# First pair of batches: order of one x load, of two copies and of four vector sums changed

## The chip, the cores and the metric

The kernel runs on one core of one Trainium2 chip. The metric is the device time of one execution in microseconds. The core has five engines that run side by side, each with a queue of its own: PE multiplies matrices into PSUM, DVE, ACT and POOL do elementwise work, SP only issues DMAs. An instruction waits in its queue until what it needs is there, and all behind it on that engine wait too.

## The reference

```python
def _attn_ref(x, state):                     # x (8,8,512,64), state (8,8,32,64)
    scores = scale * np.matmul(x, state.transpose(0, 1, 3, 2))
    ...                                      # softmax over the last axis
    xread = np.matmul(a, state)
    scores2 = scale * np.matmul(state, x.transpose(0, 1, 3, 2))
    ...                                      # softmax over the last axis
    sread = np.matmul(a2, x)
    return np.concatenate([xread, sread], axis=2)

def _moe_ref(x, w_in, w_out):                # w_in (512,2048), w_out (2048,512)
    h = x @ w_in
    g = h * np.cos(h)
    return (g @ w_out).astype(np.float32)
```

The attention's result, 544 rows of 512 numbers for each of eight batches, goes row by row through the second function. The two weight matrices arrive as float64, so the kernel gets them as pairs of 32-bit words.

## The kernel before

**Tiles and steps.** The order of all work is written out by hand. The main loop (line 1283) goes through 16 steps for each of the eight batches, and 16 more for the rows of the states. A step makes one tile: 128 of the 2048 columns of h for one batch's 512 rows. Its parts are `hidden` (PE, the matmuls of h, line 490), `gate` (ACT, a rounding of h, line 560), `gate2` (DVE, q, line 563), `gate3` (ACT, the cosine as a sine, line 566) and `gate4` (DVE, the product g = h cos h, line 580). Batches go in pairs of 32 steps. In the first 28 steps h goes to two PSUM banks in turn, so `hidden` of a step needs `gate4` of two steps before. `first_pair` (line 1186) is the order of a step in these; `later_pair` is that of the steps after.

**A batch's attention** is spread over the steps by `plan` (lists `pe`, `x_act`, `y_act`, `x_dve`, `y_dve`, `z_act`, which `first_pair` and `later_pair` call as `go(0)` to `go(5)`). It turns x (`tokens`), forms scores, maxima, exponentials and sums, spreads and normalizes them, turns the second softmax (`turn`, PE into the banks `at`; `turn_kept`, ACT, PSUM to SBUF), and reads x with it (`reads`, then `keep` on DVE). For batch 0, `turn` stands in step 1 and `reads` in steps 2 and 3. `reads` is the last to need the x of its batch in `x_b`: with it the loads of the next batch's x become due (line 478), and `load_now` (line 128) issues them on SP at the end of the step.

**Weights.** Eighteen loads bring float64 weights into three buffers in turn (`fetch`, SP, line 212). `convert` makes float32 of each in parts: "1" and "2" on ACT (lines 243 and 246), "b" and "c" on DVE (249 and 252), "f" on POOL (257), which also issues the load that can follow (a buffer is free after "c"). Step 0 has conversion 4, step 1 conversion 5, and so on (`conv_at`).

**Products with seven multiplications.** From step 29 on, h times w_out is made with seven block products in place of eight, twice nested. That needs sums of weights and of gates:
- inner sums of seven weight matrices (`inner_weights`, POOL, line 681). Each also sends its matrix (`send_raw`, line 669) and its four sums (line 684) to HBM with SP, and `fetch_block` (line 700) reads them back block by block; the first three at step 24. The last of the seven, matrix `SQ`, is itself a difference of two weight matrices, made by `weight_sum` on DVE in two halves (L1108, 128x1024 each, at the ends of steps 22 and 25), and its `inner_weights` stands in step 25.
- outer sums of gates (`outer_sum`, through `sub`, line 709), in halves `half` and pieces `i`. On DVE a piece is one instruction of 128x1024, on POOL two of 128x512. For the first pair, `mid_at` puts a sum into the middle of a step (after `go(3)`), `outer_at` at its end. The sum `o=0, x1=0, x2=2` has half 0 in steps 25 and 26 (`mid_at`) and half 1 at the ends of steps 26 and 28, all on DVE.
- inner sums of gates for each product (`Product.sums`, POOL, line 709), in steps 27 to 29 for the first.
- sums of the attention's weights (`sw_sums`, POOL, line 523), which the seven products of h (line 540) need from step 30 on; POOL does them after the first two of those inner sums of gates.

`warm` (line 938) is matmuls of zeros that PE does while it would wait.

Of the kernel before, what the change touches and what calls it, by code (L numbers as in the profile page):

```python
# [13 lines left out]
ALU = mybir.AluOpType  # L14
# [8 lines left out]
def kernel(  # L23
# [55 lines left out]
    def matrix(n):  # L79
        return quad(n).rearrange("p t (u d) -> p (t u) d", d=HD)  # L80
# [142 lines left out]
    def convert(i, parts):  # L223

        for p in parts:
            if p == "f":
                if i not in (1, 2) and i + 3 < N_LOADS:  # L230
                    fetch(max(i + 4, 6))
            elif f64:
                convert_part(i, p)
# [30 lines left out]
    class Attention:  # L264
# [144 lines left out]
                                    in_=self.z2[:, j, P * c:P * c + P],  # L409
                                    identity=ident)  # L410

        def turn_kept(self, j):
            nc.scalar.copy(self.a2T[:, j].rearrange("p c m -> p (c m)"),
                           at[j])

# [557 lines left out]
    def plan(b):  # L975
        pe, x_act, y_act, x_dve, y_dve, z_act = [
            {s: [] for s in range(NF)} for _ in range(6)]

        def prod(s, b, nt, *bank):
            pe[s].append((b, "products", nt) + bank)  # L980
            x_act[s].append((b, "products_kept", nt) + bank)

        def pairs(s, b, name, kept, i):
            pe[s] += [(b, name, i), (b, name, i + 1)]
            x_act[s].append((b, kept, i))
            y_act[s].append((b, kept, i + 1))

        def early(b, s):
            if b == 1:
                pairs(s[0], b, "tokens", "tokens_kept", 0)  # L990
                pairs(s[1], b, "tokens", "tokens_kept", 2)
            else:
                for k in range(NK):
                    to = (x_dve, y_dve)[k % 2]
                    to[s[k // 2]].append((b, "tokens_turned", k))
            pe[s[2]].append((b, "scores"))
            x_dve[s[2]].append((b, "max1"))
            x_dve[s[3]].append((b, "spread1"))
            y_dve[s[3]].append((b, "shift"))
            if b == 1:  # L1000
                x_dve[s[4]].append((b, "max2"))
                y_act[s[4]].append((b, "exps"))
            else:
                y_dve[s[4] - 1].append((b, "max2"))
                z_act[s[4]].append((b, "exps"))
            if b == 1:
                x_dve[s[5]].append((b, "sums"))
                y_dve[s[5]].append((b, "spread1"))
                x_dve[s[6]].append((b, "norm1"))
            else:  # L1010
                y_dve[s[4]].append((b, "sums1"))
                x_dve[s[5]].append((b, "spread2"))
                y_dve[s[5]].append((b, "norm1"))

        def late(b, s):
            pairs(s[0], b, "turn", "turn_kept", 0)
            pe[s[1]].append((b, "reads", 0))
            pe[s[2]].append((b, "reads", 1))
            x_dve[s[2]].append((b, "keep"))
            if len(s) > 3:  # L1020
                turned(b, s[3])

        def turned(b, s):
            pe[s].append((b, "keep2"))
            x_act[s].append((b, "keep3"))


        if b == 0:
            pe[0].append((0, "products", 0, SIDE, HC, WC))
            y_dve[0] += [(0, "products_taken", 0, SIDE, HC, WC),  # L1030
                         (0, "inverse2")]
            prod(7, 0, 2, SIDE)
            prod(11, 0, 3)
            prod(13, 1, 0, SIDE)
            late(0, (1, 2, 3, 4))
            early(1, (5, 6, 7, 8, 9, 10, 11))
            late(1, (12, 13, 14))
        else:
            bank = (SIDE,) if b == 1 else ()
            if b == 1:  # L1040
                turned(1, 0)
            prod(0, b, 1, *bank)
            prod(3, b, 2, *bank)
            prod(8, b, 3, *bank)
            if b + 1 < B:
                prod(12, b + 1, 0)
                early(b + 1, (1 + (b == 1), 2 + (b == 1), 4, 5, 7, 8, 9))
                late(b + 1, (9, 10, 11, 15))
        return pe, x_act, y_act, x_dve, y_dve, z_act
# [6 lines left out]
    for i, t in enumerate(all_tiles):  # L1056
        t.mate = all_tiles[i ^ 1]
    pairs = [all_tiles[2 * NF * n].pair for n in range(B // 2)]
    stage_at, sums_at, outer_at, mid_at, weights_at = [
        defaultdict(list) for _ in range(5)]  # L1060
    PERIOD, STAGES = 2 * NF, len(ORDER)
    ROWS = {"p1": 0, "p2": 1, "p5": 0, "p3": 3, "p6": 0, "p7": 2, "p4": 1}

# [23 lines left out]
    for n in range(B // 2):  # L1087
        end = n == B // 2 - 1
        for r, engine, o, x1, x2, half in (
                ((25, 26), dve, 0, 2, 0, 0),  # L1090
                ((27 - (not n), 28), dve, 0, 2, 0, 1), ((31, 31), pool, 2, 3, 2, 0), ((33, 33), dve, 0, 3, 0, 0),
                ((34, 34 + (not end)), dve, 0, 3, 0, 1),
                ((35, 36), dve, 2, 3, 2, 1),
                ((38 - end,) * 2, pool, 1, 1, 0, 0),
                ((39 - end,) * 2, pool, 1, 1, 0, 1)):
            for i in range(2):
                at_ = mid_at if n == 0 and r[i] < 27 and r[0] == 25 else outer_at
                at_[PERIOD * n + r[i]].append(
                    (engine, n, o, x1, x2, half, i))

# [31 lines left out]
            0, a11, temps[0], (i,), () if i < 3 else (16,) * 4))  # L1132
    for steps, o, x1, x2, op in (
            ((18, 19), A21, A11, A21, ALU.subtract),
            ((22, 25), SQ, A12, A22, ALU.subtract)):
        for i in range(2):
            weights_at[steps[i]].append(
                lambda o=o, x1=x1, x2=x2, op=op, i=i: weight_sum(
                    o, x1, x2, op, i))

# [5 lines left out]
    for at_, what in (  # L1146
            (15, lambda: send_raw(0, a11)),
            (17, lambda: send_raw(2, a22)),
            (19, lambda: send_raw(1, a12)),
            (15, lambda: quads_free.append(10)),  # L1150
            (16, lambda: pool_sum(SQ, A21, A22, ALU.add)),
            (17, lambda: quads_free.append(9)),
            (17, lambda: inner_weights(3, matrix(SQ), temps[1])),
            (18, lambda: pool_sum(A22, SQ, A11, ALU.subtract)),
            (20, lambda: inner_weights(5, matrix(A21), temps[0])),
            (22, lambda: inner_weights(4, matrix(A22), temps[1])),
            (23, lambda: quads_free.append(A11)),
            (25, lambda: inner_weights(6, matrix(SQ), temps[0])),
            (25, lambda: quads_free.append(A21)),
            (27, lambda: quads_free.append(A22)),  # L1160
            (27, lambda: quads_free.append(TEMPS)),
            (28, lambda: quads_free.append(SQ))):
        weights_at[at_].append(what)
# [18 lines left out]
    def go(n):  # L1182
        for p in todo[n]:
            part(*p)

    def first_pair(step, t):
        last, conv = conv_at.get(step - 1, -1), conv_at.get(step, -1)
        if step == 4:
            warm(1, acc[0])
        if step != 1:  # L1190
            hidden(t)
        if step == 0:
            hidden(all_tiles[1])
            warm(3, acc[0])
            gate(t)
            gate2(t)
            convert(3, "bcdf")
            convert(4, "1")
            go(0)
        else:  # L1200
            go(0)
            if step == 5:
                states(1, side_banks[0])
            gate(t)
            gate2(t)
            if step == 3:
                warm(4, acc[0])
                part(0, "products", 1, SIDE)
            go(1)
            go(3)  # L1210
            for what in mid_at[step]:
                outer_sum(*what)
            if step == 1:
                convert(4, "bcdf")
            elif last >= 0 and step < 5:
                convert(last, "bcdf")
            if conv >= 0 and not todo[1]:
                convert(conv, "1")
        gate3(t)
        go(5)  # L1220
        if step == 3:
            part(0, "products_kept", 1, SIDE)
        gate4(t)
        if step == 6:
            states_kept(1, side_banks[0])
        if last >= 0 and 4 < step < 11:
            convert(last, "bcdf")
        if conv >= 0 and todo[1] and step > 0:
            convert(conv, "1")
        go(2)  # L1230
        if conv >= 0:
            convert(conv, "2")
        if step > 10 and conv >= 0 and not todo[1]:
            convert(conv, "bcdf")
        go(4)
        if step > 10 and conv >= 0 and todo[1]:
            convert(conv, "bcdf")
# [126 lines left out]
```

## Time and profile before

| | us |
|---|---|
| median of 9 runs (lowest, highest) | 743.95 (743.48, 745.67) |
| the profiled execution | 744.91 |
| its span in the profile | 743.1 |
| PE busy | 713.1 |
| POOL busy | 538.9 |
| DVE busy | 498.2 |
| ACT busy | 338.7 |

The rows below have, per stretch of the profile, each engine's busy time:

| stretch, us | steps | PE | DVE | ACT | POOL |
|---|---|---|---|---|---|
| 24 to 60 | 0 to 6 | 34.34 | 24.63 | 30.80 | 14.35 |
| 60 to 104 | 7 to 16 | 38.93 | 37.45 | 36.71 | 23.88 |
| 104 to 126 | 16 to 22 | 20.93 | 18.61 | 10.33 | 20.80 |
| 126 to 160 | 22 to 30 | 27.87 | 29.23 | 18.49 | 24.44 |
| 160 to 220 | 30 to 41 | 58.34 | 44.62 | 29.53 | 56.01 |

A timeline row gives start, duration, engine, line, operation, tile written and tiles read, shape, count, and in brackets the idle time before it with the engine and line that ended it. Times are from the start of the span. TensorE's granted clock is at full speed (0.999 of it) throughout.

### The profile page before, as it was taken

The page shows a single profiled execution, that of the slowest core. Times are in us where ns is not written, and L with a number is a line of the kernel's source. Part 1 is how long each engine was busy: PE and PEld are TensorE (multiplying, and loading weights), DVE is VectorE, ACT ScalarE, POOL GpSimd, SP SyncE. Part 2 cuts the span into 40 slices and gives each one's busy share as a digit, 9 for nine tenths or more (in the row PEclk, how much of TensorE's full clock was granted, in tenths as well). Part 3 has the DMA queues.
Part 4 walks back from the last instruction along what each step waited for, and adds up shares of the span by engine and source line. Part 5 has one row for each costly group of instructions (what it writes and reads, how often), then busy time and mean ns, then how long its engine had stood idle before and what let it go on. Part 6 is the DMA issues. An engine that isn't in the chain of part 4 may idle for free.

```text
span 743.1 us, 10759 instructions
## 1 busy us (share of the span) xinstructions
PE 713.1 (96%) x3624; PEld 519.8 (70%) x3624; DVE 498.2 (67%) x707; ACT 338.7 (46%) x562; POOL 538.9 (73%) x528
## 2 busy tenths in 40 slices
PE   8999989799999999999999999999999999999997
PEld 4443333367767878777777778777688788888886
DVE  4768779876975658859766587869656457355550
ACT  3777873644373446344634454443734433211110
POOL 1345469598998997497998765779989665799600
PEclk9999999999999999999999999999999999999999
DMA  9495399977245964692237725762325466455662
GB/s 252 148 257 202 133 242 304 315 158 166 76 127 116 212 157 132 143 194 83 86 86 149 177 86 112 144 170 72 75 73 122 114 201 143 111 155 195 166 149 43
DMA packets 212470, 112.39 MB, mean 151 GB/s; under 512 B 158336, under 2 KB 175232, under 8 KB 212416
## 3 DMA queue, kind: packets, MB, share of 16 engines
q1 hardware_dynamic: 211328, 111.19, 57.8%
q8 instruction: 29, 0.48, 0.3%
q10 hardware_dynamic: 960, 0.39, 0.2%
q14 instruction: 25, 0.20, 0.1%
q0 software_dynamic: 128, 0.13, 0.1%
HBM read 88.08 MB, written 23.59 MB: 150 GB/s over the span
## 4 chain that ended last, share of the span: by engine, by line
PE 57%; POOL 22%; DVE 8%; ACT 4%; DMA 4%; issue 3%; SPq 1%; POOLq 0%; DVEq 0%; ACTq 0%
PE o L762 29%; POOL g_all L709 17%; PE h L540 13%; PE h L490 5%; POOL swS_all L523 3%; PE at L328 3%; PE at L863 2%; DMA x_b<-in_x_dram 2%; POOL sw L523 2%; DVE g_all L709 2%; PE at L425 2%; PE o L938 1%; DVE q_all L563 1%; PE o L863 1%; DVE g_all L580 1%
## 5 line engine op out<-in xcount | busy, mean ns | idle before, releaser
L709 POOL TENSOR_TENSOR g_all<-g_all 128x512 f32<-128x512 f32 x256 | 336.4, 1344 | 55.2 <-DVE g_all L709 40.1
L762 PE MATMUL o<-g_all 128*128 128x256 f32 x1456 | 344.0, 381 | 2.4 <-POOL g_all L709 2.4
L762 PEld LDWEIGHTS o<-g_all 128*128 128x128 f32 x1456 | 273.8, 190 | 49.2 <-issue 5.5
L563 DVE TENSOR_TENSOR q_all<-q_all,h 128x1024 f32<-128x1024 int32 (+1 forms) x88 | 85.5, 971 | 48.6 <-ACT q_all L560 48.4
L566 ACT ACTIVATE q_all<-q_all,halfpi 128x1024 f32<-128x1024 f32 (+1 forms) x88 | 84.1, 956 | 54.9 <-DVE q_all L563 54.8
L560 ACT ACTIVATE q_all<-h 128x1024 int32<-128x1024 f32 (+1 forms) x88 | 73.2, 831 | 77.6 <-PE h L540 35.1
L580 DVE TENSOR_TENSOR g_all<-h,q_all 128x1024 f32<-128x1024 f32 (+1 forms) x88 | 85.7, 973 | 26.7 <-ACT q_all L566 24.8
L549 DVE TENSOR_TENSOR h<-h,sums_all 128x256 f32<-128x256 f32 x96 | 41.2, 429 | 76.1 <-PE h L540 58.2
L490 PE MATMUL h<-aT,sw 128*128 128x512 f32 x128 | 61.6, 605 | 10.9 <-DVE g_all L580 10.2
L540 PE MATMUL h<-aS_all,swS_all 128*128 128x256 f32 x192 | 60.3, 396 | 3.2 <-ACT sums_all L544 1.8
L540 PE MATMUL h<-aT,sw 128*128 128x256 f32 x192 | 59.6, 392 | 3.8 <-DVE g_all L580 3.4
L540 PE MATMUL h<-aS_all,sw 128*128 128x256 f32 x192 | 58.0, 384 | 0.1
L709 DVE TENSOR_TENSOR g_all<-g_all 128x1024 f32<-128x1024 f32 x40 | 57.1, 1444 | 0.1
L540 PEld LDWEIGHTS h<-aS_all,swS_all 128*128 128x128 f32 x192 | 33.9, 189 | 27.9 <-issue 11.2
L490 PEld LDWEIGHTS h<-aT,sw 128*128 128x128 f32 x128 | 22.8, 189 | 43.3 <-DVE g_all L580 19.3
L767 ACT COPY o<-o 128x256 f32<-128x256 f32 x26 | 9.3, 357 | 85.3 <-PE o L762 85.3
L257 POOL TENSOR_TENSOR w_in<-w_in,aS_all 128x1024 int32<-128x1024 int32 (+1 forms) x10 | 19.3, 1927 | 37.9 <-DVE w_in L252 17.9
L540 PEld LDWEIGHTS h<-aT,sw 128*128 128x128 f32 x192 | 34.5, 190 | 16.3 <-DVE g_all L580 12.1
L523 POOL TENSOR_TENSOR swS_all<-sw 128x128 f32<-128x128 f32 x48 | 22.8, 474 | 29.2 <-ACT sw L461 29.2
L540 PEld LDWEIGHTS h<-aS_all,sw 128*128 128x128 f32 x192 | 35.6, 190 | 8.3 <-DVE h L549 2.7
L773 ACT COPY o<-sums_all 128x256 f32<-128x256 f32 x26 | 9.8, 378 | 68.9 <-PE o L762 68.9
L603 DVE SCALAR_TENSOR_TENSOR held<-o,held 128x512 f32<-128x512 f32 x40 | 27.1, 680 | 13.7 <-PE o L762 13.1
(115 smaller groups left out, 919.7 us busy)
## 6 DMA issues: line engine op xcount, KB each, us to landing
g_all<-blocks_kept SPq DMA_DIRECT2D x206, 256.0 KB, 2.9
blocks_kept<-g_all SPq DMA_DIRECT2D x48, 256.0 KB, 3.4
g_all<-in_moe_w_out_dram SPq DMA_DIRECT2D x8, 1024.0 KB, 5.0
out_dram<-ot SPq DMA_DIRECT2D x128, 64.0 KB, 2.0
g_all<-in_moe_w_in_dram SPq DMA_DIRECT2D x6, 1024.0 KB, 5.6
xT<-in_x_dram SPq DMA_DIRECT2D x96, 64.0 KB, 3.0
x_b<-in_x_dram SPq DMA_DIRECT2D x24, 256.0 KB, 4.8
x_b<-in_x_dram SPq DMA_DIRECT2D x16, 128.0 KB, 4.4
```

Of the source, the lines that this page charges most:

```text
L328: nc.tensor.matmul(out=(to or at)[j][Ns * k:Ns * k + Ns, n0:n1], lhsT=w[D * j:D * j + D, self.b, Ns * k:Ns * k + Ns], rhs=r(slice(D * j, D ...
L490: nc.tensor.matmul(out=t.hp, lhsT=t.lhs(i), rhs=t.rhs(i), start=(i == 0), stop=(i == t.kn - 1))
L523: nc.gpsimd.tensor_tensor(o, x1, x2, op=op)
L540: nc.tensor.matmul(out=out_, lhsT=w, rhs=r, start=start, stop=True, skip_group_check=True)
L549: nc.vector.tensor_tensor(o, h2[:, LO], sums_all[:, 0], op=ALU.add)
L560: nc.scalar.activation(t.q.bitcast(I32), t.hp, func=ACTF.Copy, bias=0.25)
L563: nc.vector.tensor_tensor(t.q, t.q.bitcast(I32), t.hp, op=ALU.subtract)
L566: nc.scalar.activation(t.q, t.q, func=ACTF.Sin, bias=halfpi, scale=-TWO_PI)
L580: nc.vector.tensor_tensor(g, t.hp, t.q, op=ALU.mult)
L603: nc.vector.scalar_tensor_tensor(out=out.t[:, ch], in0=bank, scalar=TWO_PI, in1=b.t[:, ch], op0=ALU.mult, op1=ALU.add)
L709: engine.tensor_tensor(o[:, i:i + n], x1[:, i:i + n], x2[:, i:i + n], op=ALU.subtract)
L762: nc.tensor.matmul(out=o, lhsT=ring[(self.first + k) % NB][:, i], rhs=g[:, i], start=(start and i == 0), stop=(i == QT - 1), skip_group_ch ...
```

## The change

Four edits, all for the first pair of batches:

1. At step 3 `load_now(H)` stands right after `go(0)`, where `reads` of batch 0 has just been issued, and not only at the end of the step. On SP the eight loads of batch 1's x now stand ahead of weight load 9 (into w_out), not behind it.
2. For batch 0 the turned weights are copied out of PSUM by DVE (`turn_taken`), not by ACT. On DVE the first copy stands between `gate2` and conversion 4's part "b" of step 1, the second behind `gate4` of step 1. On ACT conversion 5's part "1" now stands ahead of step 1's sine.
3. The two halves of the last `weight_sum` move to step 23: the first into the new list `idle_at`, which is called behind `gate4` and ahead of `go(4)` (the reduction of the exponentials, `sums1`), the second to the end of step 23. The `inner_weights` that reads them, with its four DMAs (`send_raw`), moves from step 25 to 24, ahead of the first three block fetches on SP; its four sums on POOL follow those of matrix 4, as before.
4. Half 1 of the outer sum `o=0, x1=0, x2=2` goes from DVE (ends of steps 26 and 28) to POOL (end of step 25), there four instructions of 128x512 behind the last `inner_weights` and ahead of the first inner sums of gates.

PE has the same instructions in the same order.

```diff
-        def turn_kept(self, j):
-            nc.scalar.copy(self.a2T[:, j].rearrange("p c m -> p (c m)"),
-                           at[j])
+        def turn_kept(self, j, copy=None):
+            (copy or nc.scalar.copy)(
+                self.a2T[:, j].rearrange("p c m -> p (c m)"), at[j])
+
+        def turn_taken(self, j):
+            self.turn_kept(j, nc.vector.tensor_copy)
...
         def late(b, s):
-            pairs(s[0], b, "turn", "turn_kept", 0)
+            if b == 0:
+                pe[s[0]] += [(b, "turn", 0), (b, "turn", 1)]
+                x_dve[s[0]].append((b, "turn_taken", 0))
+                y_dve[s[0]].append((b, "turn_taken", 1))
+            else:
+                pairs(s[0], b, "turn", "turn_kept", 0)
...
+    idle_at = defaultdict(list)
...
-                ((27 - (not n), 28), dve, 0, 2, 0, 1), ((31, 31), pool, 2, 3, 2, 0), ((33, 33), dve, 0, 3, 0, 0),
+                ((27, 28) if n else (25, 25), dve if n else pool, 0, 2, 0, 1),
+                ((31, 31), pool, 2, 3, 2, 0), ((33, 33), dve, 0, 3, 0, 0),
...
-                at_ = mid_at if n == 0 and r[i] < 27 and r[0] == 25 else outer_at
+                at_ = (mid_at if n == 0 and r[0] == 25 and engine is dve
+                       else outer_at)
...
-            ((22, 25), SQ, A12, A22, ALU.subtract)):
+            ((23, 23), SQ, A12, A22, ALU.subtract)):
         for i in range(2):
-            weights_at[steps[i]].append(
+            (idle_at if o == SQ and i == 0 else weights_at)[steps[i]].append(
...
-            (25, lambda: inner_weights(6, matrix(SQ), temps[0])),
+            (24, lambda: inner_weights(6, matrix(SQ), temps[0])),
...
             go(0)
+            if step == 3:
+                load_now(H)
...
             convert(conv, "2")
         if step > 10 and conv >= 0 and not todo[1]:
             convert(conv, "bcdf")
+        for what in idle_at[step]:
+            what()
         go(4)
```

## The prediction

> **What bounds the kernel now.** I read the page's busy shares, then the windows table, then the timelines of the first 180 us engine by engine, then the chain of waits. PE has 713.1 us of work in a span of 743.1 us, and the change leaves PE's instructions and their order alone: time can come only out of PE's 30 us of waits. The windows put 1.66 us of them in 24 to 60 us and 6.13 us in 126 to 160 us, the two stretches that the change works in.
>
> First stretch: rows of the timelines of SP, PE and ACT (start, duration, engine, line, operation; in brackets the wait before it and what ended it).
>
> ```profile
> 42.95 0.37 SPq L212 DMA_DIRECT2D g_all<-in_moe_w_out_dram  x1
> 43.42 6.17 SPq L131 DMA_DIRECT2D x_b<-in_x_dram  x8
> ...
> 49.38 0.63 PE L287 MATMUL at<-ident,x_b 128*128 128x128 f32 x4 [0.24 <-DMA x_b<-in_x_dram]
> 50.68 0.63 PE L287 MATMUL at<-ident,x_b 128*128 128x128 f32 x4 [0.67 <-ACT xT L296]
> ...
> 55.27 0.60 ACT L560 ACTIVATE q_all<-h 128x512 int32<-128x512 f32 x1 [1.38 <-PE h L490]
> ```
>
> Batch 1's x stands on SP behind a weight load that waits for a conversion. PE loses 0.24 and 0.67 us at the turns of that x, and ACT then waits 1.38 us for PE.
>
> Second stretch, timelines of DVE, POOL and PE:
>
> ```profile
> 127.44 1.83 DVE L1108 TENSOR_TENSOR g_all<-g_all 128x1024 f32<-128x1024 f32 x1
> 129.20 0.68 DVE L563 TENSOR_TENSOR q_all<-q_all,h 128x512 f32<-128x512 int32 x1
> ...
> 142.16 1.21 DVE L1108 TENSOR_TENSOR g_all<-g_all 128x1024 f32<-128x1024 f32 x1
> ...
> 146.33 1.69 DVE L709 TENSOR_TENSOR g_all<-g_all 128x1024 f32<-128x1024 f32 x1
> ```
> ```profile
> 143.45 6.92 POOL L681 TENSOR_TENSOR g_all<-g_all 128x512 f32<-128x512 f32 x4 [8.01 <-DVE g_all L1108]
> ```
> ```profile
> 131.41 1.98 PE L490 MATMUL h<-aT,sw 128*128 128x512 f32 x4 [1.85 <-DVE g_all L580]
> ...
> 138.83 1.98 PE L490 MATMUL h<-aT,sw 128*128 128x512 f32 x4 [1.83 <-DVE g_all L580]
> ...
> 142.29 1.98 PE L490 MATMUL h<-aT,sw 128*128 128x512 f32 x4 [0.46 <-DVE g_all L580]
> ...
> 149.77 1.09 PE L328 MATMUL at<-w_in,st_all 64*32 64x512 f32 x16 [0.84 <-DVE sr L435]
> ...
> 157.23 0.70 PE L540 MATMUL h<-aS_all,swS_all 128*128 128x256 f32 x2 [0.57 <-POOL swS_all L523]
> ```
>
> DVE bounds here. PE waits for DVE's gate products (L580), and DVE does weight and outer sums that nobody needs yet ahead of the gate of a later step. POOL sits idle for 8.01 us until DVE's last weight sum. What PE gains here must also get past the next stage, where the chain of waits (start, duration, engine, tile, line) runs on POOL from 180.74 on:
>
> ```profile
> 179.56 1.12 DVE g_all L709
> ...
> 208.44 10.84 POOL g_all L709 x8
> ...
> 219.75 0.70 PE h L540 x2
> ```
>
> That POOL stretch begins behind a DVE sum, which stands behind a gate whose sine on ACT waited for PE's stage ending at 175.36. So it begins earlier by what PE gains by then, and POOL, fed by nothing later, hands the gain on to the end.
>
> **Turned weights read back by DVE (steps 1 and 2).** Two ACT copies (0.58 us each, L413) become two DVE copies; the near row is DVE's COPY of 128x512 from PSUM, 0.69 us alone and about 0.6 in a row of work. PE has the turns done at 31.3, so the copies wait for nothing. DVE is full here: the first copy stands before the gate product of step 1, which moves from 33.84 to 34.44, so PE's tile at 34.58 (already waiting 0.43 for it) moves by +0.6. The fixed matmuls behind it (warm-ups, products) carry +0.6 to 45.4, where PE waited 0.32 for POOL: +0.28 is left. ACT wins little: its sine of step 1 still waits for DVE, but its gate of step 2 comes 1.5 us earlier, so DVE's q of step 2 comes at 35.65 in place of 35.93 and POOL's conversion of step 3 starts about 0.4 earlier. Alone this part is between 0 and +0.6; I take +0.28 at step 4.
>
> **x issued ahead (step 3).** The eight issues go behind PE's last read of batch 0's x (38.1 with the +0.6) and the weight load issued at 38.56, so they start at about 38.9 and take 6.17 us as before, to 45.1. All of x lands by about 48. PE's turns then start at 49.3 and 49.9 (50.68 before): -0.75. The tile of step 6 ends at 54.25 and ACT's gate of it starts at 54.3 in place of 55.27, with ACT free by 54.1; DVE's q, which followed directly at 55.90, and the chain behind it move by 0.85 to 0.95. I take **-0.85** for the stretch, the DVE copies in it. What is moved past: the weight load issued at 42.95 now goes at 45.2. It landed after 5.1 us; the DMA engines were idle from 43.1 to 44.9, so x fills that hole, and 1 MB of it at the 220 to 240 GB/s that the rows show takes until 47.8, the weights at 410 GB/s another 2.6: landed at 50.4. ACT converts it at 51.5 (51.21 before). Cover 1.1 us; past it each us costs one, and at 2.3 us late the whole gain of x is gone. The load behind it waited for SP until 49.70 and goes earlier. Bounds of the part: +0.3 to -1.0.
>
> **Last weight sum (steps 22 and 25 to 23).** Without the 1.83 at 127.44, q of step 23 starts at 127.44 (its ACT input is long there): the gate product of step 23 and PE's tile at 131.41 come 1.76 earlier. The first half sum now runs beside ACT's table load and exponentials (three us in which DVE was idle 1.68), hidden. The second half sum stands ahead of q of step 24: exponentials end at 131.27, the reduction takes to 132.55, the sum to 134.3, so q of step 24 starts there and not at 135.09; the gate product of step 24 follows 2.46 us of spread work, at 136.76 for 138.08: **-1.32**. At step 25 the sum at 142.16 is gone: another -1.1 from q of step 26 on. POOL's four sums of the last weights (and SP's four raw sends with them, now ahead of the first three block fetches, which then go some 3 us later, at about 142, needed at 149) start when POOL is free, 135.44, and not at 143.45.
>
> **Half an outer sum to POOL.** Two DVE sums (1.69 at 146.33, 1.48 at 153.68) become four POOL instructions of 128x512, 1.28 us each by the row of such sums alone, 1.73 by the row of 6.92 for four; their operands (gates of steps 4 to 7 and 20 to 23) are long there, so they wait only for the four last-weight sums ahead of them on POOL. The first one stood before q of step 27: with it gone that q comes 1.6 earlier still, no longer behind DVE but behind PE's own tile. The 0.84 at 149.77 (keep, behind the late q) goes.
>
> **Contention, where a rule speaks against this.** POOL's 8 us hole covered DVE's longest sums. Filled, it takes their quiet. Rows: a DVE sum of 128x1024 takes 1.21 or 1.22 with POOL idle (142.16, 140.42), and 1.18, 2.18, 1.83, 1.91, 1.69, 1.48 with POOL busy, mean 1.71. The Trainium skill, "SBUF — State Buffer", section "Who interferes with whom", says that a DVE instruction with two SBUF inputs and a GpSimd one that reads SBUF exclude each other for a whole instruction. Two such DVE instructions on the path (the norm of step 24, the outer sum of step 25) lose their quiet: by the rows +0.5 each, together +1.0; by the rule up to a whole POOL instruction each, 2.5. I take the rows: most instances lie far from a full wait.
>
> **Sum of the second stretch.** PE's tile at 142.29: -1.32 + 1.0 = -0.3. The gates of steps 26 and 27, without the sums of 142.16 and 146.33, no longer hold PE, whose own rows then follow without a gap: 141.99, 143.91, 144.93, 146.75, 148.6 (products, 149.77 before), 149.6, 151.45, 153.2, 154.9, and 155.3 for the pair at 157.23: **-1.9**, the three waits of 0.3, 0.84 and 0.57 with the pipeline's restarts of some 0.1. Without any contention it is -2.9, with the rule's -0.4. POOL must have its first weight piece (swS, L523) by then: it is free at 134.6 with the first stretch's shift (135.44 - 0.85), and last weights 6.3, outer sum 5.8, first sums of the next product 5.6 and the piece 0.65 make 152.9, against 155.3 - 0.85 = 154.5. It holds by 1.6 us.
>
> Total: -0.85 - 1.9 = -2.75. On the profiled execution (744.91, of which 743.1 is the span) that is 742.15; the median of the runs lies 0.96 below the profiled one, so 743.95 becomes **741.2**.
>
> **Rivals.**
> *A. The forecast*, 740.1 to 742.7: the two stretches as above, from no contention with all of x's gain (-0.95 - 2.9) to the rule's contention (-0.85 - 0.4). Chance 0.72.
> *B. Only the second stretch counts*: the weight load moved past lands late and eats x's gain, or DVE's copies do. For it: DVE is full at 31 to 36 us, and the cover is 1.1 us. Against: the DMA hole at 43.1. Time 743.95 + 0.1 - 1.2 = about 742.8, with the second's value halfway between row and rule. Chance 0.14.
> *C. POOL becomes the bound: slower.* Between 134.5 and PE's L540 POOL now has twelve sums in place of eight, then swS. It is later than before once a sum takes over 1.83 us on average (134.6 + 12 x 1.83 + 0.65 = 157.2, where PE stood before). A single such sum took up to 2.36 (into aS_all at 112.33) and 2.25 (117.23): at 2.2 throughout, swS comes at 161.7, PE stands 4.4 us later than before and the time is about 748.4. For it: the lock rule, and that POOL bounds the next 60 us. Against: the mean of four in a busy stretch is 1.73. Chance 0.09.
> *D. The change is absorbed*: PE's earlier tiles meet another wait of the same length (the block fetches, issued some 3 us later, or the load of the next tokens), 743.9. Against: SP has no wait left in its list then, and the fetches have 4 us to spare. Chance 0.05.
>
> About 0.2% (1.5 us) is what this measurement tells from no change. Faster by more, under 742.45: A but for its top, and a third of B, 0.77; within: the rest of A, B and D, 0.14; slower: C and the bad end of B, 0.09. Range for 8 in 10: 739.9 to 742.9, A and most of B.
>
> **What would show it.** In the profile after: x_b issues at about 39 with the wait at L287 gone; the copies of L413 on DVE and PE's tile of step 3 at 35.2; PE's stall before the tile of step 25 down from 1.85 to nearly nothing; POOL busy without the 8 us hole from 105 to 155; no stall at the products of step 28; PE's first L540 pair on aS_all near 154.5. Wrong if POOL's swS ends that last stall, if ACT waits for a weight load at step 5, or if DVE's 128x1024 sums from 130 to 145 go over 2 us.

## The result, and the profile after

| | before | after |
|---|---|---|
| median of the runs taken side by side, us | 744.60 | 741.99 (741.57 to 743.18) |
| ratio, 95% interval | | 0.9968 [0.9960, 0.9976] |
| the same pair once more, us | 744.63 | 742.82 (741.45 to 745.11) |
| ratio, 95% interval | | 0.9971 [0.9955, 0.9987] |
| span of the profiled execution | 743.1 | 739.8 |
| start of PE's tile of step 0 in it | 23.08 | 21.70 |

Two of the 31 runs of before took 2575 us, for a cause that no run here shows; without them its median is 744.53. By the ratios, which are taken from the fast runs, the kernel became faster by 2.2 to 2.4 us (by the medians alone 2.6 and 1.8). The two spans differ by 3.3 us, but 1.38 of that lies ahead of the tile of step 0, where both kernels have the same work; in the other profiles of this study that tile starts anywhere from 21.78 to 22.84. So times are counted from that tile below, and of the span's 3.3 us the change has 1.92. Up to line 412 the line numbers of after are those of before; then they are 3 higher, and `weight_sum` is at L1119.

First stretch. SP's timeline of the kernel after (start, duration, engine, line, operation, tiles, count) and PE's, which has the wait before the row in brackets:

```profile
38.00 6.18 SPq L131 DMA_DIRECT2D x_b<-in_x_dram  x8
44.28 0.51 SPq L212 DMA_DIRECT2D g_all<-in_moe_w_out_dram  x1
```
```profile
33.79 1.98 PE L493 MATMUL h<-aT,sw 128*128 128x512 f32 x4 [1.03 <-DVE g_all L583]
...
47.89 1.04 PE L287 MATMUL at<-ident,x_b 128*128 128x128 f32 x8
...
50.92 1.88 PE L493 MATMUL h<-aT,sw 128*128 128x512 f32 x4
```

The eight issues of x stand ahead of weight load 9, and the turns at L287 wait for nothing. The wait for DVE's gate product at the tile of step 3 has grown from 0.43 to 1.03: these are the DVE copies. The tile of step 6 (50.92) is at 29.22 counted from the tile of step 0, where before it was at 30.22.

Second stretch. PE, DVE and POOL of the kernel after:

```profile
127.31 1.98 PE L493 MATMUL h<-aT,sw 128*128 128x512 f32 x4
...
136.34 3.41 PE L493 MATMUL h<-aT,sw 128*128 128x512 f32 x4 [3.43 <-DVE g_all L583]
...
140.70 1.98 PE L493 MATMUL h<-aT,sw 128*128 128x512 f32 x4
...
147.27 1.09 PE L328 MATMUL at<-w_in,st_all 64*32 64x512 f32 x16
...
153.98 0.59 PE L543 MATMUL h<-aS_all,swS_all 128*128 128x256 f32 x2
```
```profile
127.17 2.24 DVE L1119 TENSOR_TENSOR g_all<-g_all 128x1024 f32<-128x1024 f32 x1
129.33 1.29 DVE L341 TRANSPOSE_TENSOR_REDUCE i<-aT 128x16 f32<-128x512 f32 x2
130.55 2.30 DVE L1119 TENSOR_TENSOR g_all<-g_all 128x1024 f32<-128x1024 f32 x1
...
133.38 0.65 DVE L384 TENSOR_SCALAR i<-i 128x34 f32<-128x34 f32 x1
...
135.63 0.65 DVE L583 TENSOR_TENSOR g_all<-h,q_all 128x512 f32<-128x512 f32 x1
136.20 1.42 DVE L402 TENSOR_TENSOR aT<-aT,xT 128x1024 f32<-128x1024 f32 x1
...
138.14 1.69 DVE L712 TENSOR_TENSOR g_all<-g_all 128x1024 f32<-128x1024 f32 x1
...
141.08 2.21 DVE L712 TENSOR_TENSOR g_all<-g_all 128x1024 f32<-128x1024 f32 x1
```
```profile
127.05 1.28 POOL L684 TENSOR_TENSOR aS_all<-g_all 128x512 f32<-128x512 f32 x1
128.41 2.13 POOL L684 TENSOR_TENSOR aS_all<-aS_all,g_all 128x512 f32<-128x512 f32 x1
...
131.73 2.25 POOL L684 TENSOR_TENSOR aS_all<-g_all,aS_all 128x512 f32<-128x512 f32 x1
133.94 7.03 POOL L684 TENSOR_TENSOR g_all<-g_all 128x512 f32<-128x512 f32 x4
140.94 10.87 POOL L712 TENSOR_TENSOR g_all<-g_all 128x512 f32<-128x512 f32 x8
151.77 0.64 POOL L526 TENSOR_TENSOR swS_all<-sw 128x128 f32<-128x128 f32 x1
```

Read PE first. The waits of 1.85, 0.46, 0.84 and 0.57 are gone, but that of 1.83 has become 3.43: what PE gained at the tile of step 25 it waits away at the tile of step 26, for the gate product of step 24 (135.63). DVE tells why. That product stands behind both halves of the weight sum, and these took 2.24 and 2.30 us. POOL's rows beside them are the four sums of matrix 4, and of each pair that overlaps one row is drawn out to some 2.2 us.

### The profile page after: what moved, and what is told of

The parts are those of the page before. It is cut to its first block, busy times and chain, and to the rows that moved or that the text cites. A ratio compares the mean times of both kernels' runs of the same rounds, so it can differ in the third digit from the quotient of the medians.

```text
span 739.8 us, 10756 instructions
## 1 busy us (share of the span) xinstructions
PE 712.2 (96%) x3624; PEld 518.7 (70%) x3624; DVE 499.4 (68%) x707; ACT 338.2 (46%) x560; POOL 545.8 (74%) x532
## 4 chain that ended last, share of the span: by engine, by line
PE 61%; POOL 22%; DVE 8%; issue 3%; ACT 3%; DMA 2%; SPq 1%; POOLq 0%; DVEq 0%; ACTq 0%
PE o L765 29%; POOL g_all L712 16%; PE h L543 13%; PE h L493 7%; POOL swS_all L526 3%; PE at L328 3%; PE at L866 2%; PE at L428 2%; POOL sw L526 2%; PE o L637 1%; DMA x_b<-in_x_dram 1%; PE o L941 1%; DVE q_all L566 1%; PE o L866 1%; DVE i L341 1%
## 5 line engine op out<-in xcount | busy, mean ns | idle before, releaser
L712 POOL TENSOR_TENSOR g_all<-g_all 128x512 f32<-128x512 f32 x260 | 342.3, 1348 | 55.3 <-DVE g_all L712 40.2
L493 PE MATMUL h<-aT,sw 128*128 128x512 f32 x128 | 63.1, 617 | 10.9 <-DVE g_all L583 10.2
L543 PE MATMUL h<-aT,sw 128*128 128x256 f32 x192 | 59.6, 392 | 3.7 <-DVE g_all L583 3.4
L543 PE MATMUL h<-aS_all,swS_all 128*128 128x256 f32 x192 | 60.2, 395 | 2.6 <-ACT sums_all L547 1.8
L543 PE MATMUL h<-aS_all,sw 128*128 128x256 f32 x192 | 58.1, 384 | 0.1
L712 DVE TENSOR_TENSOR g_all<-g_all 128x1024 f32<-128x1024 f32 x38 | 54.8, 1460 | 0.1
L543 PEld LDWEIGHTS h<-aS_all,swS_all 128*128 128x128 f32 x192 | 33.9, 189 | 27.0 <-issue 11.3
L543 PEld LDWEIGHTS h<-aT,sw 128*128 128x128 f32 x192 | 34.5, 189 | 16.1 <-DVE g_all L583 12.0
L543 PEld LDWEIGHTS h<-aS_all,sw 128*128 128x128 f32 x192 | 35.6, 190 | 8.3 <-DVE h L552 2.7
```

The source lines that it names most:

```text
L493: nc.tensor.matmul(out=t.hp, lhsT=t.lhs(i), rhs=t.rhs(i), start=(i == 0), stop=(i == t.kn - 1))
L543: nc.tensor.matmul(out=out_, lhsT=w, rhs=r, start=start, stop=True, skip_group_check=True)
L712: engine.tensor_tensor(o[:, i:i + n], x1[:, i:i + n], x2[:, i:i + n], op=ALU.subtract)
```

## The experiments

All profiles in one table, in us from the start of PE's tile of step 0. "Pair" is PE's first pair at L543 (L540 before) on `aS_all` and `swS_all`, the end of the second stretch. The last column is the second stretch alone, from the tile of step 24 to the pair.

| kernel | step 3 | step 6 | step 12 | step 24 | pair | end | pair - step 24 |
|---|---|---|---|---|---|---|---|
| before | 11.50 | 30.22 | 58.08 | 103.58 | 134.15 | 720.02 | 30.57 |
| after | 12.09 | 29.22 | 57.10 | 102.61 | 132.28 | 718.10 | 29.67 |
| after_again | 12.10 | 29.22 | 57.24 | 103.75 | 132.20 | 718.73 | 28.45 |
| x_ahead | 11.50 | 28.94 | 57.05 | 102.55 | 133.13 | 719.43 | 30.58 |
| copies | 12.09 | 30.54 | 58.43 | 103.93 | 134.51 | 720.32 | 30.58 |
| no_copies | 11.49 | 28.93 | 57.91 | 103.44 | 133.28 | 719.22 | 29.84 |
| sums | 11.50 | 30.20 | 58.06 | 103.58 | 133.47 | 719.12 | 29.89 |
| weight_sum | 11.50 | 30.42 | 58.30 | 103.79 | 134.74 | 720.66 | 30.95 |
| outer_pool | 11.50 | 30.59 | 58.46 | 104.95 | 138.71 | 726.98 | 33.76 |
| pool_quiet | 12.09 | 29.20 | 57.09 | 102.59 | 131.18 | 718.00 | 28.59 |
| warm_gap | 12.11 | 29.23 | 57.17 | 103.69 | 132.16 | 718.22 | 28.47 |
| hybrid | 12.09 | 29.21 | 57.74 | 104.24 | 134.36 | 721.62 | 30.12 |

One profile per kernel stands in it: differences of some 0.4 us are what it can't tell apart, since rows of the same code differ by as much (before, weight_sum and outer_pool have 30.22, 30.42 and 30.59 at step 6).

### The edits of the first stretch: x_ahead, copies, no_copies

x_ahead is the kernel before with only edit 1:

```diff
             go(0)
+            if step == 3:
+                load_now(H)
```

> The kernel before with the early issue of batch 1's x alone (load_now at step 3); DVE's copies and the moved sums left as before. Theory (the x issue gives the whole gain of the first stretch, the DVE copies cost a little): the turns of x follow PE's tile of step 5 without a wait, ACT's gate of step 6 is 1.3 to 1.4 us earlier than before counted from the tile of step 0 (the complete change has 1.0), and that stays to step 22; in all -1.3 us, ratio about 0.998. Rival (the copies on ACT are what lets the gain through, ACT being late for the conversions): no more than 0.3 us earlier at step 6. Rival (the weight load moved behind x lands late): ACT waits for a DMA before part 1 of conversion 9.

Measured: 743.33 us against 744.54, ratio 0.9986 [0.9977, 0.9995]; the tile of step 6 is 1.28 us earlier, that of step 12 only 1.03. Rows of the timelines of x_ahead, ACT's with their waits: ACT at load 9, SP's issue of load 9, ACT at load 12:

```profile
50.95 1.16 ACT L243 ACTIVATE g_all<-g_all 128x1024 f32<-128x1024 f32 x1 [0.64 <-DMA g_all<-in_moe_w_out_dram]
```
```profile
44.34 0.52 SPq L212 DMA_DIRECT2D g_all<-in_moe_w_out_dram  x1
```
```profile
64.00 1.17 ACT L243 ACTIVATE g_all<-g_all 128x1024 f32<-128x1024 f32 x1 [0.66 <-DMA g_all<-in_moe_w_out_dram]
```

Weight load 9, issued at 44.34 behind x, has not landed when ACT comes to convert it: ACT waits 0.64, and the load takes 6.6 us where such a load took 5.1 before. PE doesn't feel this at once: up to the tile of step 10 the 1.28 stands. But the conversion of load 9 ends later, and its POOL part issues load 12. That one goes 0.31 us later than in after, counted from the tile of step 0 (36.84 for 36.53), ACT waits 0.66 for it at 64.00, and the tile of step 11 is the first that has lost 0.25 of the 1.28.

copies is the kernel before with only edit 2 (the diff of `turn_taken` and `late` shown with the change).

> The kernel before with DVE's copies of the turned weights alone. Theory: PE's tile of step 3 comes 0.6 us later than before counted from the tile of step 0, the product of step 4 still 0.3 later, and the wait for x at step 5 absorbs it: no change of the time, within 0.1 us. Rival (the copies help by themselves because ACT becomes free): step 6 earlier than before by 0.3 us or more.

Measured: 744.44 us, ratio 0.9999 [0.9991, 1.0008]. The tile of step 3 is 0.59 later, as in the forecast; 0.32 is left at step 6 and 0.35 at step 12.

no_copies is the kernel after with edit 2 undone:

```diff
-            if b == 0:
-                pe[s[0]] += [(b, "turn", 0), (b, "turn", 1)]
-                x_dve[s[0]].append((b, "turn_taken", 0))
-                y_dve[s[0]].append((b, "turn_taken", 1))
-            else:
-                pairs(s[0], b, "turn", "turn_kept", 0)
+            pairs(s[0], b, "turn", "turn_kept", 0)
```

> The change whole, but batch 0's turned weights are copied by ACT again, as before the change. If the copies cost only where x still stands behind weight load 9: counted from the tile of step 0, the tile of step 3 stands at 11.5 (12.1 with the copies), that of step 6 at 28.9 (29.2), that of step 12 at 57.05 (57.1), and the time is that of the changed kernel within 0.1% (0.997 of before). If the copies are needed for x to come early: step 6 at 29.5 or later and the time 0.6 us above the changed kernel's.

Measured: 742.66 us beside 742.82 of the changed kernel on the same chip, ratios 0.9969 and 0.9971. Steps 3 and 6 are as the first case says. Step 12 is not: at 57.91 it is 0.81 later than in after, as load 9 was 1.22 us late; 0.5 of it goes at the tiles of steps 7 and 8, the rest at that of step 11, ahead of which ACT waits 1.07 for load 12:

```profile
51.63 1.17 ACT L243 ACTIVATE g_all<-g_all 128x1024 f32<-128x1024 f32 x1 [1.22 <-DMA g_all<-in_moe_w_out_dram]
```

What follows: x issued ahead is the whole gain of the first stretch, and its price is load 9, which landed 6.3 to 7.2 us after its issue in the five profiles in which ACT waited for it (0.31 us in warm_gap, 0.40 in after_again, 0.57 in hybrid, 0.64, 1.22), and no later than 6.05 in after and 6.03 in pool_quiet, where ACT didn't wait. The copies make no difference that the times show, alone or beside the rest. They bring ACT to load 9 some 0.4 us later, so they may cover part of its lateness; but hybrid has them too, and there the tile of step 12 is still 0.64 later than in after. With one profile each that stays open.

### The edits of the second stretch: sums, weight_sum, outer_pool

sums is the kernel before with edits 3 and 4; weight_sum has edit 3 alone, outer_pool edit 4 alone. The lines that tell them apart:

```diff
 # weight_sum (edit 3)
-            ((22, 25), SQ, A12, A22, ALU.subtract)):
+            ((23, 23), SQ, A12, A22, ALU.subtract)):
...
-            (25, lambda: inner_weights(6, matrix(SQ), temps[0])),
+            (24, lambda: inner_weights(6, matrix(SQ), temps[0])),
 # outer_pool (edit 4)
-                ((27 - (not n), 28), dve, 0, 2, 0, 1), ((31, 31), pool, 2, 3, 2, 0), ((33, 33), dve, 0, 3, 0, 0),
+                ((27, 28) if n else (25, 25), dve if n else pool, 0, 2, 0, 1), ((31, 31), pool, 2, 3, 2, 0), ((33, 33), dve, 0, 3, 0, 0),
```

> The kernel before with the moved weight sum and the outer sum on POOL, x and copies as before. Theory (two waits of PE of 1.85 and 1.83 us join into one of about 3.4, TensorE's clock falls to half in it in some executions and takes 1.6 us back): -0.9 us where the granted clock falls below 1 around step 26, -2.5 where it stays, median about -1.5 (ratio 0.998); DVE's two last weight sums take about 2.2 us each. Rival (contention alone, as forecast): -1.9 in all executions, no dip of the clock, weight sums 1.7 to 1.8 us.

Measured for sums: 744.25 us, ratio 0.9993 [0.9984, 1.0003]. In its profile the second stretch gains 0.68, with weight sums of 2.24 and 2.30 as in after.

> The kernel before with the moved last weight sum alone (and its sums on POOL at step 24); the outer sum stays on DVE. Theory: PE's wait before step 26 is about 3.4 us, the wait before the products of step 28 stays because the outer sum still stands ahead of step 27's gate on DVE; nothing or less gained, 0 to -0.6 us. Rival (the weight sum alone makes the gain of the second stretch): -1 us or more.

Measured for weight_sum: 744.06 us, ratio 0.9993 [0.9980, 1.0005], and the second stretch 0.38 longer than before. The tile of step 26 is not earlier behind that of step 24 than in after (12.02), and TensorE's granted clock then stays at half from 137.6 to some 144: the tile of step 27 starts 1.51 us behind the gate product that it needs. DVE waits 0.40 for ACT behind that, so the low clock may hold all of the 0.38. The outer sum still stands on DVE ahead of the gate of a later step (1.91 us at 146.11), and the first inner sums on POOL wait for its second piece. POOL's timeline of weight_sum:

```profile
155.16 1.27 POOL L712 TENSOR_TENSOR g_all<-g_all 128x512 f32<-128x512 f32 x1 [5.72 <-DVE g_all L712]
```

> The kernel before with half of the outer sum on POOL at step 25 and the weight sum where it was. Theory (POOL becomes the bound, the forecast's case C): POOL starts the sums of the last weights at 143.4 as before, then has four sums more, so its first swS comes at about 162 and PE's pair of L540 waits 4 us longer than before: +4 us, 748 to 749, ratio 1.005. Rival (POOL has room): no change or faster.

Measured for outer_pool: 750.32 us, ratio 1.0067 [1.0046, 1.0089], slower by 5.0 us by the ratio (5.75 by the medians). Timelines of outer_pool, POOL and PE:

```profile
143.57 5.95 POOL L681 TENSOR_TENSOR g_all<-g_all 128x512 f32<-128x512 f32 x4 [9.25 <-DVE g_all L1109]
149.48 10.41 POOL L709 TENSOR_TENSOR g_all<-g_all 128x512 f32<-128x512 f32 x8
159.85 0.63 POOL L523 TENSOR_TENSOR swS_all<-sw 128x128 f32<-128x128 f32 x1
```
```profile
160.53 1.22 PE L540 MATMUL h<-aS_all,swS_all 128*128 128x256 f32 x2 [4.67 <-POOL swS_all L523]
```

POOL takes the outer sum, but starts only at 143.57, when DVE has made the last weight sum at its old place; its sums of 1.36 us each then end with `swS` 4.67 us too late for PE. In after the same twelve sums start at 133.94. What follows: neither edit is shown to be worth anything without the other, and edit 4 alone costs 5 us. Edit 3 lets POOL start early, edit 4 uses that.

### What the long weight sums cost: pool_quiet, hybrid, after_again

The theory: the two weight sums take 2.2 us because POOL adds beside them. pool_quiet is the kernel after without POOL's four sums of matrix 4:

```diff
-            nc.gpsimd.tensor_tensor(o, x1, x2, op=op)
+            if which != 4:
+                nc.gpsimd.tensor_tensor(o, x1, x2, op=op)
```

> The changed kernel with POOL's four sums of weight matrix 4 left out (the matrix's four sent sums are then not made, so the products that use them are wrong): POOL has nothing to do while DVE makes the last weight sum. Theory (DVE's two halves take 2.24 and 2.30 us because POOL holds what both share): both halves take 1.2 us, the small sum behind them 0.18 in place of 0.65, and PE's tile of step 26 comes about 2 us earlier than in the changed kernel counted from the tile of step 0. Rival (the halves are slow because SP's and the DMA's traffic is high there): they stay at 2.2.

Measured: 742.20 us in eight runs, ratio 0.9964 [0.9949, 0.9980]. DVE's timeline of pool_quiet:

```profile
127.56 1.21 DVE L1120 TENSOR_TENSOR g_all<-g_all 128x1024 f32<-128x1024 f32 x1
...
130.54 1.18 DVE L1120 TENSOR_TENSOR g_all<-g_all 128x1024 f32<-128x1024 f32 x1
...
132.25 0.87 DVE L384 TENSOR_SCALAR i<-i 128x34 f32<-128x34 f32 x1
```

With POOL idle both take 1.2, PE's tile of step 26 comes 1.31 us earlier (113.33 for 114.64 in after), and the second stretch gains 1.98 where after gains 0.90. That is the long sums' cost at this place, and it is less than the 2 us of the forecast. At the end little of it is left in this profile (718.00 for 718.10 in after), and the times of the two overlap: 0.35 is lost near 257 us, and about 0.6 behind PE's last product. The small instruction at L384 stayed long (0.87), since POOL's next four sums began at 131.81, beside it.

hybrid is the kernel after with the second half of the weight sum on POOL, ahead of matrix 4's sums, and one piece of the outer sum back on DVE:

```diff
-        nc.vector.tensor_tensor(o_, x1_, x2_, op=op)
+        if o == SQ and i == 1:
+            for j in range(2):
+                nc.gpsimd.tensor_tensor(o_[:, j], x1_[:, j], x2_[:, j], op=op)
+        else:
+            nc.vector.tensor_tensor(o_, x1_, x2_, op=op)
...
+                e = dve if n == 0 and r == (25, 27) and i else engine
```

> The changed kernel with the second half of the last weight sum on POOL (two sums, ahead of those of matrix 4) and one of the two outer pieces back on DVE at the end of step 27, so that POOL has as many sums as in the changed kernel. Theory (DVE's last weight sum ahead of step 24's gate is what eats the gain): the tile of step 26 comes 1.7 us earlier than in the changed kernel, POOL's swS is then what PE's pair waits for, and the time is 0.5 to 1.5 us under the changed kernel (740.5 to 741.5). Rival (POOL's two sums ahead of matrix 4 push swS back): 742 or above.

Measured: 742.32 us, ratio 0.9962 [0.9949, 0.9976], level with after, so the gain of 0.5 to 1.5 us over it didn't come. The tile of step 26 comes 10.42 us after that of step 24 (12.03 in after), but PE then waits 1.05 for DVE's next gate product, and DVE's outer piece (2.15 at 147.85) still stands among its products; PE's tile behind the wait took 3.31, at a granted clock of 0.50. The profile is that of its slowest run (745.30). No version of this study is shown to beat the changed kernel.

after_again is the changed kernel once more.

> The changed kernel once more, beside no_copies on one chip. If the profile of after was typical: ratio 0.996 to 0.998, both weight sums at 2.2 to 2.3 us, tile of step 26 12.0 us behind that of step 24, PE's pair on aS_all 29.7 us behind it. If the long weight sums were one execution's phase between DVE and POOL: sums of 1.2 to 1.7, and the pair at 28.5.

Its time says the first case, its profile the second. DVE's timeline of after_again:

```profile
128.48 1.22 DVE L1119 TENSOR_TENSOR g_all<-g_all 128x1024 f32<-128x1024 f32 x1
130.24 1.30 DVE L341 TRANSPOSE_TENSOR_REDUCE i<-aT 128x16 f32<-128x512 f32 x2 [0.55 <-ACT aT L366]
131.47 1.67 DVE L1119 TENSOR_TENSOR g_all<-g_all 128x1024 f32<-128x1024 f32 x1
```

Here the first sum is hidden (DVE then still waits 0.55 for ACT), and the second stretch gains 2.12. But this profile is 1.14 us late at the tile of step 24, and comes to the pair at 132.20, as after does at 132.28. The delay arises between the tiles of steps 20 and 21. Rows of DVE and POOL there, first in after, then in after_again:

```profile
110.01 1.18 DVE L1119 TENSOR_TENSOR g_all<-g_all 128x1024 f32<-128x1024 f32 x1
```
```profile
109.97 2.36 POOL L684 TENSOR_TENSOR aS_all<-g_all 128x512 f32<-128x512 f32 x1
```
```profile
110.33 2.30 DVE L1119 TENSOR_TENSOR g_all<-g_all 128x1024 f32<-128x1024 f32 x1
```
```profile
110.28 1.27 POOL L684 TENSOR_TENSOR aS_all<-g_all 128x512 f32<-128x512 f32 x1
```

The two start within 0.05 us of each other in both. In one execution DVE has its 1.18 and POOL 2.36, in the other POOL its 1.27 and DVE 2.30: one works, the other waits it out. This is a matter of chance and not of the change (a draw, in what follows): outer_pool, whose code up to there is that of before, lost it too (2.29). Where DVE loses, PE takes 46.5 us from the tile of step 12 to that of step 24, else 45.5, but DVE then meets POOL in another phase and both weight sums are shorter (1.21 and 1.67 in warm_gap, as above in after_again). From the tile of step 12 to the pair both ways cost about the same: 75.18 in after, 74.96 in after_again, 74.99 in warm_gap, where before took 76.07. So the second stretch gains 0.9 to 1.1 net in these three; sums and no_copies, which have edits 3 and 4 too and did not lose the draw, gain 0.66 and 0.70 (75.41 and 75.37).

No profile of before has the draw lost, but outer_pool has, and up to the tile of step 27 it does what before does. From the tile of step 12 to that of 27 it takes 62.14, before 61.13: there the lost us is not made good, while the changed kernel takes 61.90 with the draw won and 61.68 and 61.70 with it lost. If that held up to the pair, the change would be worth some 2.1 us in executions that lose the draw (76.07 + 1.01 - 74.97). That is an estimate; no run here shows it.

### What the joined wait costs: warm_gap

In after PE's tile behind the wait of 3.43 took 3.41 in place of 1.98. Windows of after over it (busy us of PE, PEld, DVE, ACT, POOL with the number of instructions, then the granted clock, the DMA share and GB/s):

```profile
136.30:138.00 1.70, 1.67 (x2) 0.84 (x3) 1.70 (x2) 0.29 (x1) 1.70 (x2) 0.50 1.03 380
138.00:139.70 1.70, 1.70 (x5) 0.37 (x3) 1.70 (x2) 1.45 (x3) 1.70 (x2) 0.64 1.00 300
```

TensorE's granted clock is at half. The rival theory: this, and not the long sums, takes back the gain. warm_gap is the kernel after with three matmuls more, which fill the wait:

```diff
+        if step == 26:
+            for _ in range(3):
+                nc.tensor.matmul(out=side_banks[0], lhsT=ident,
+                                 rhs=w_in[:, 0, 0:WC], start=True, stop=True)
```

> The changed kernel with three matmuls of 128x512 ahead of the tile of step 26, into a PSUM bank that nothing uses then; what they make is not used. Theory (the joined wait lets the clock fall): the granted clock stays at 1.00 around step 26, the tile of step 26 takes 1.9 and not 3.4 us, and the time is about 1 us under the changed kernel in the mean (741.0 for 742.0), up to 1.6 under an execution with the dip. Rival (the long tile of step 26 is something else, its operands or a modelled end): the tile stays at 3.4 us and the time at 742 or above it, as the three matmuls may push the tile back.

Measured: 742.53 us, ratio 0.9976 [0.9964, 0.9988]. PE's timeline of warm_gap:

```profile
136.88 1.98 PE L493 MATMUL h<-aT,sw 128*128 128x512 f32 x4
138.91 1.09 PE L428 MATMUL at<-x_b,xT 128*64 128x128 f32 x16
141.05 1.12 PE L493 MATMUL h<-aT,sw 128*128 128x512 f32 x2 [1.05 <-DVE g_all L583]
```

The tile takes 1.98 again, and PE then waits 1.05 for DVE's gate product of step 25. In after that product ended at 140.44 and PE's slowed work at 140.70: the low clock cost at most 0.26 us there. In no_copies, sums and pool_quiet, where the clock fell at the same tile, the tile of step 27 starts 0.40, 0.46 and 0.46 behind that gate product, in weight_sum 1.51; with the clock at full speed it is 0.05. (In warm_gap, as in after_again, the second stretch is short because the weight sums are.) In after, then, the rival falls as the main cause: the low clock explains a few tenths, the long sums 1.02.

## Why the prediction was right, and where it was off

- **Copies by DVE.** +0.6 at the tile of step 3 became +0.59, +0.28 behind it +0.30 (tile of step 5: 24.48 for 24.18).
- **x issued ahead.** -0.85 became -1.00 at the tile of step 6 and -0.98 at that of step 12 (-0.84 in after_again). The mis-sized term is "Cover 1.1 us" for the load moved past: it is nothing (after) to 1.2 us short (no_copies), because the load takes up to 7.2 us behind x (at most 6.05 in after) and not the 5.2 that the forecast made from the 220 to 240 GB/s and 410 GB/s. The "wrong if ACT waits for a weight load at step 5" did show, with 0.40 in after_again, where it took 0.14 us; in no_copies it left 0.17 us of 1.29 at the tile of step 12, which is rival B's case in full. The hole of the DMA engines was also shorter than the forecast read it: their busy share was 0.02 only from 43 to 44, and 0.70 and 0.43 in the two halves of the next us. So the gain of this part, right in both profiles of the changed kernel, had no cover; that it came is in part luck.
- **Last weight sum.** The stall of 1.85 ahead of the tile of step 25 went, as forecast. The gate product of step 24, -1.32 in the forecast (10.10 us behind its tile), came at 11.32 in after and 10.30 in after_again (11.42 before).
- **Contention, the term that was off.** The forecast gave it +1.0, on the two instructions that lose POOL's 8 us hole. Those were about right: the norm took 1.42 and the outer sum 1.69, together +0.7 over the 1.21 of a quiet POOL. But the moved weight sums were taken as hidden and at 1.75, though the change puts them beside POOL's sums of matrix 4. They took 2.24 and 2.30, not far from 1.21 and a whole POOL instruction of 1.26 in a row. In after this is 0.40 on the first sum that nothing hid (the reduction at L341 starts 5.02 us behind the tile of step 24, in after_again 4.62) and 0.63 more on the second: the 1.02 between the two executions' gate products. The reason given, "most instances lie far from a full wait", averages over a mixture: a row of 1.2, one of 1.7 and one of 2.3 are no sample around a mean, but who came first. For the rows that overlap a POOL sum from its start, the rule in the Trainium skill, "SBUF — State Buffer", section "Who interferes with whom" (two SBUF inputs on DVE and a GpSimd instruction that reads SBUF shut each other out for a whole instruction), is what the pairs 1.18 with 2.36 and 2.30 with 1.27 show.
- **Second stretch.** -1.9 became -0.9 in after, -2.1 in after_again, -2.0 in pool_quiet; with what the draw at step 20 gives or takes, 0.7 to 1.1 net. What was off lies ahead of the tile of step 27: forecast 0.3 earlier, it came 0.76 later in after, counted from the tile of step 24 (16.39 for 15.63). From there to the pair 14.94 became 13.28, and the forecast's own tiles give 13.3: the waits of 0.84 and 0.57 went as it said.
- **POOL.** The margin of `swS`, 1.6 us, was 1.57 (152.41 for 153.98). Its twelve sums took 1.49 us each, under the 1.83 from which rival C decides. That PE can come to wait for POOL's `swS` is what outer_pool shows, but there because POOL starts late and not, as C has it, because its sums are long.
- **To the end.** From the pair on, 585.87 us before and 585.82 in after: the gain is handed on whole. In after_again it is 586.53: at 255.75 PE waits 0.45 for a block fetch (`g_all<-blocks_kept`) and comes out 0.72 later than after does there. hybrid loses as much at the same product, x_ahead 0.36, after nothing. So whether a gain gets past this place differs from one profile to the next; the forecast had no term for it, and its rival D, which named the block fetches, is true of a part.

In sum the profile of after has -1.00 and -0.90, a span shorter by 1.92 for a forecast of 2.75, and that of after_again one by 1.29, while the ratios say 2.2 and 2.4. What makes up the difference stays open; both spans lie within the intervals of the ratios, and the draw at step 20, as estimated above, would go in that direction. The time came within the range, but the forecast of the second stretch is right only where the weight sums happen to be short: that the total fits so well is in part luck.

## What to carry to other kernels

Before moving a long DVE sum of two SBUF inputs, look which POOL instruction runs beside its new place, and price it with a whole one of these: the same sums took 1.21 and 1.18 with POOL idle, 2.24 and 2.30 beside it. A producer that moves earlier and its consumer's new place on another engine belong together; one without the other gained nothing that the times show here, or lost 5 us. And one profile of a kernel whose engines meet by chance says little of one stretch: take the sum over a longer stretch, and more than one profile.

## What was not expected of the hardware

- **The draw between DVE and POOL.** In twelve profiles the DVE sum at step 20 took 1.18 eight times and 2.29 or 2.30 four times, nothing between. POOL's row starts 0.03 to 0.05 us ahead of DVE's where DVE has its way and 0.05 to 0.06 ahead where POOL has. If the starts decide, it is by a hundredth or two. Losing costs PE 1.0 us in each of the four.
- **A wait can halve TensorE's clock.** Behind the wait of 3.43 in after the clock was 0.50 for the next 1.7 us and 0.64 for the 1.7 after. Much shorter waits did it too: ahead of the tile of step 25, behind 1.86 in outer_pool and in x_ahead, the clock fell to 0.50 and the tile took 3.46 and 3.56, while behind 1.85 in before it took 1.98; ahead of that of step 26, behind 2.14 in pool_quiet it took 2.94, behind 2.41 in after_again 1.98. A window that runs free of the program, as the Trainium skill has it ("TensorE: Matmul & The Clock Gate", Part 1), would explain that equal waits differ; no run here shows the window itself. At the next tile that waits for DVE it costs only what PE's slower work lasts beyond that wait: 0.26 us in after, 1.51 in weight_sum.
